# Four edits to the first half of a fused attention and two-layer-block kernel: later exponentials and casts, one copy joined, six staging tiles

## The chip, the cores and the metric

One core of a Trainium2 chip runs the whole program. The metric is device time in microseconds (us) of one execution. The kernel before took 992.32 us (median of 3 runs, 990.58 to 995.51).

## The reference

Three stages follow one another. (1) Causal attention with forgetting, for 4 batches of 8 heads, 576 tokens, head size 64: scores are `q·k / 8` plus a decay `cum[i] - cum[j]` (`cum` is the running sum of `log f`), the upper triangle is masked, and each row is turned into weights by `exp(score - row max)`, divided by its sum, and multiplied with `v`. (2) With the heads side by side (2304 tokens of 512): `h = x @ w_in` (2048 wide), `g = h * tanh(softplus(h))`, `x = g @ w_out`. (3) `a = x @ w1`, `b = x @ w2` (1024 wide each), `out = ((a * b) @ w3) @ w_out2`. All weights of the two blocks come as 64-bit floats and are turned into 32-bit ones on the chip.

## The kernel before

**Two halves.** `phase_a` does the attention of 16 pairs of heads, converts all weights, multiplies w3 with w_out2 beforehand, and computes `h = x @ w_in` for three of the four batches. `phase_b` computes `h` for the last batch and then the rest of blocks (2) and (3) on token quarters. The change is in the first half; the second is touched only where both halves share `l1_unit`.

**Slots.** The first half is a loop over 68 slots, four for each pair of heads `p` (lines 675 to 706, the four are numbered j = 0 to 3). A head's rows are cut into five blocks, called c = 0 to 4; a score block c has 128 rows of both heads, the last has 64 rows of each head in one tile. In slots j = 0, 1, 2 the scores of blocks (0, 1), (2, 3) and (4) are computed. At the end of slots j = 1, 2, 3 and of the next pair's slot 0, `turn` transposes blocks (0, 1), (2), (3) and (4) on TensorE and copies them out of PSUM. So a block is transposed a slot or more after its exponentials. In slot j = 3 the product with `v` (`pv`) of the pair before is made, scaled by VectorE (`x_rows`), and split into a high and a low part (`x_parts`: two casts on ScalarE, two subtractions on GpSimd).

**Fillers.** TensorE's order is written out by hand. Between scores and transposes each slot runs filler matmuls in two bursts (lines 697 to 702). From slot 21 on they are first-layer units: 12 matmuls give one 128 x 288 block of `h` in one of two PSUM banks (`ps_l`), ScalarE copies it into a staging tile `h`, and SyncE stores the tile to memory (`h_scr`). There are two units in a slot, one for each burst, 24 matmuls of line 512. There are `HB = 3` staging tiles. A unit can start only when the unit two before it has been copied out of its bank.

**Softmax of a block.** Line 357 (363 and 364 for block 4): VectorE adds the mask, scales and takes the row minimum. Line 367: ScalarE takes the exponential in place and sums the row (an ACTIVATE and a read of the accumulator). Both are called from `score`, before the first filler burst.

**Conversions.** Each 1024-word piece of a weight is loaded into a raw tile (line 117, four buffers of the tag `cvr`, names cvrt for w3, cvri for w_in, cvru for w_out, cvrv for w1 and w2), ScalarE makes the exponent part (line 132, `cv_exp`), VectorE puts the bits together (lines 140 to 142, `cv_bits`), and then the raw tile is free. `job` puts the load at slot s-1 and the two steps one or two slots after s. The loads go over SyncE's queue, together with the stores of `h`. From slot 47 on one load is issued for each buffer that comes free.

**Order on the other engines.** The orders of ScalarE, VectorE, GpSimd and SyncE are fixed when the program is built: a planner goes through it in time with estimated durations, and when an engine is free it takes the ready instruction with the highest priority. Priority is the place in the program, moved ahead by an offset: 200 for the scores, the softmax and `cv_exp`, 150 for the copies of `h`, 100 for the transposes and their copies, 50 for `pv`, `x_rows` and `x_parts`. On the chip each engine then works strictly in that order.

**First-layer order of batch 0.** `l1_all` takes both halves of the tokens for the first `L1_BOTH = 10` weight columns m, then half 0 of the remaining six, then half 1 of them.

Of the kernel before, what the change touches and what calls it, by code (L numbers as in the profile page):

```python
# [9 lines left out]
F32 = mybir.dt.float32  # L10
F32R = mybir.dt.float32r
BF16 = mybir.dt.bfloat16
I32 = mybir.dt.int32
AF = mybir.ActivationFunctionType
# [10 lines left out]
TB = S // 2  # L25
# [10 lines left out]

HB = 3
CV = 4
HP_L1 = 150
HP_ATT = 100  # L40
HP_SM = 200
HP_PV = 50
# [3 lines left out]
W3_STEP = 1.14  # L46
WP_END = 21
W_IN_SLOT = 16
L1_BOTH = 10
W_IN_STEP = 0.8  # L50
W_OUT_SLOT = 30
W_OUT_STEP = 1.08
# [22 lines left out]
class Kernel:  # L75
# [38 lines left out]

    def cv_load(self, key, src, where=None):
        if where is None:
            raw = self.att.tile([128, 1024], I32, name=f"cvr{key}", tag="cvr", bufs=4)
        else:
            raw = self.w_tile(where, f"cvr{key}", I32)
        dst = raw if len(src.shape) == 2 else raw.rearrange("p (c w) -> p c w", c=src.shape[1])  # L120
        self.nc.sync.dma_start(dst, src)
        self.cv[key] = [raw, None]

    def cv_exp(self, key):
# [3 lines left out]
        else:  # L128
            t = self.att.tile([128, 512], F32, name=f"cv{key}", tag="cv", bufs=CV)
        self.cv[key][1] = t  # L130
# [209 lines left out]
                mm(ps[:, 512 * part:512 * part + TB], t[:, LAST:LAST + 128], t[:, TB * part:TB * part + TB],  # L340
                   start=first, stop=not first)

    def softmax(self, p, c):
        nc = self.nc
        ps = self.S.pop((p, c))
        if c == 0:
            self.sums = self.att.tile([128, 16], F32, name=f"sum{p}", tag="sum", bufs=2)
        ttr = nc.vector.tensor_tensor_reduce
        self.nsm = self.nsm % 6 + 1
        st = [self.sums[:, 8 + self.nsm:9 + self.nsm]]  # L350
        if c < 4:
            n = 128 * (c + 1)
            P = self.P[c]
            self.nsm = self.nsm % 6 + 1
            st.append(self.sums[:, 8 + self.nsm:9 + self.nsm])
            for hh in range(2):
                dve = ttr(P[hh][:, :n], ps[:, 512 * hh:512 * hh + n], self.m1[:, 512 - n:], -0.125, 3.0e38, ALU.add,
                          ALU.min, st[hh])
            cols = (c, 5 + c)
        else:  # L360
            n = S
            P = self.P[4]
            ttr(P[0][:, :TB], ps[:, :TB], self.m1[:, :TB], -0.125, 3.0e38, ALU.add, ALU.min, self.sums[:, 15:16])
            dve = ttr(P[0][:, TB:n], ps[:, 512:512 + TB], self.m4, -0.125, self.sums[:, 15:16], ALU.add, ALU.min, st[0])  # L364
            cols = (4,)
        for t, b, i in zip(P, st, cols):
            ins = nc.scalar.activation(t[:, :n], t[:, :n], AF.Exp, bias=b, scale=-1.0, accum_out=self.sums[:, i:i + 1])  # L367
        return ins, dve

    def inv_sums(self):  # L370

# [39 lines left out]
    def pt_parts(self, p, c, hh):  # L411

        nc = self.nc
        copy = nc.vector.tensor_copy if hh else nc.scalar.copy
        dst = self.pt[:, 2 * (p % 2) + hh]
        if c < 4:
            o = self.t_col(c)
            src = self.ps_t[hh][:, o:o + 128 * (c + 1)].rearrange("p (k q) -> p k q", q=128)
            return copy(dst[:, 0:c + 1, 128 * c:128 * c + 128], src)  # L419
        src = self.ps_t[0].rearrange("p (k q) -> p k q", q=128)  # L420
        if not hh:
            copy(self.pt4[p % 2][0:64], self.ps_t[1][0:64, 0:128])
        return copy(dst[:, :, 512:576], src[:, :, 64 * hh:64 * hh + 64])

    def pv(self, p):
        mm = self.nc.tensor.matmul
# [38 lines left out]
    def wp_unit(self, f):  # L465
# [5 lines left out]
        def step(g, k, i):  # L471
# [7 lines left out]
            if i == 23:  # L479
                t = self.cv[2, f % 4, f // 4] = self.w_tile(0, f"wp{f}", F32)[:, :512]  # L480
                with self.tc.high_priority(offset=HP_L1):
                    self.nc.scalar.copy(t, o)
# [17 lines left out]
    def l1_unit(self, b, m, half):  # L500
        mm = self.nc.tensor.matmul
        steps = []
        box = []

        def step(c, k, i):
            if i == 0:
                box.append(self.l1_bank())
            o = box[0]
            a, bb = MM_PAIRS[k]
            w = self.wi[m][:, 512 * a + 128 * c:512 * a + 128 * c + 128]  # L510
            x = self.X[4 * b + c, half][:, TB * bb:TB * bb + TB]
            mm(o[:, :TB], w, x, start=i == 0, stop=i == 11)  # L512
            if i == 11:
                t = self.base.tile([128, TB], F32, name=f"h{b}_{m}_{half}", tag="h", bufs=HB)
                with self.tc.high_priority(offset=HP_L1):
                    if self.late_l1:
                        self.nc.vector.tensor_copy(t, o[:, :TB])
                    else:
                        self.nc.scalar.copy(t, o[:, :TB])  # L519
                self.nc.sync.dma_start(self.h_scr[128 * m:128 * m + 128, b * S + TB * half:b * S + TB * half + TB], t)  # L520

        i = 0
        for c in range(4):
            for k in range(3):
                steps.append(((f"i{m}",), lambda c=c, k=k, i=i: step(c, k, i)))
                i += 1
        return steps

    def l1_all(self, b):
        out = []  # L530
        units = [(m, half) for half in range(2) for m in range(DFF // 128)]
        if b == 0:

            units = [(m, half) for m in range(L1_BOTH) for half in range(2)]
            units += [(m, half) for half in range(2) for m in range(L1_BOTH, DFF // 128)]
        for m, half in units:
# [28 lines left out]
    def phase_a(self):  # L565
        nc = self.nc
# [55 lines left out]
        for i in range(32):  # L622
            f = i % 16
            s = W_OUT_SLOT + int(W_OUT_STEP * i)
# [7 lines left out]
            else:  # L632
                key, src = f"v{f}", self.cols((self.w1, self.w2)[f % 2], f // 2)
                job(s, key, src, self.cv_store, key, self.w12_scr[f], lag=2)
        for p in range(NPAIR):
            s = NU * p
# [8 lines left out]

        for f in FS:
            self.filler.extend(self.wp_unit(f))
        self.S, self.nsm, self.act, self.dve = {}, 0, None, None
        with self.tc.manual_schedule(engines={mybir.EngineType.PE}):
            self.slots(misc, conv, self.plan())  # L650
        self.psp.__exit__(None, None, None)
# [1 line left out]
        self.lowp.__exit__(None, None, None)  # L653

    def slots(self, misc, conv, cnt):

        def turn(p, cs):
            with self.tc.high_priority(offset=HP_ATT):
                for c in cs:
                    self.transposes(p, c)  # L660
                if cs == (4,):
                    self.nc.tensor.transpose(self.ps_t[1][0:9, 384:512], self.inv, self.ident)
                    self.inv_rows(p)
                for c in cs:
                    self.act = self.pt_parts(p, c, 0)
                    self.dve = self.pt_parts(p, c, 1)

        def score(p, cs):
            with self.tc.high_priority(offset=HP_SM):
                for c in cs:  # L670
                    self.scores(p, c)
                for c in cs:
                    self.act, self.dve = self.softmax(p, c)

        for s in range(NU * (NPAIR + 1)):
            self.slot = s
            self.done |= self.fresh
            self.fresh.clear()
            if s in L1_S:
                self.filler.extend(self.l1_all(L1_S.index(s)))  # L680
            p, j = divmod(s, NU)
            n = cnt[s]
            live = p < NPAIR
            with self.tc.high_priority(offset=HP_SM):
                for key in conv.get(s, []):
                    self.cv_exp(key)
            if live and j < 3:
                score(p, ((0, 1), (2, 3), (4,))[j])
            if p and j == (3 if live else 2):
                with self.tc.high_priority(offset=HP_PV):  # L690
                    self.pv(p - 1)
                    self.x_rows(p - 1)
                    self.x_parts(p - 1)
            with self.behind(self.dve):
                for key in conv.get(s, []):
                    self.cv_bits(key)
            k = n // 2 if s < WP_END else n // 24 * 12
            self.run_filler(k)
            with self.behind(self.act):
                for fn, a in misc.get(s, []):  # L700
                    fn(*a)
            self.run_filler(n - k)
            if p and j == 0:
                turn(p - 1, (4,))
            elif live and j:
                turn(p, ((0, 1), (2,), (3,))[j - 1])
        while self.filler and len(self.filler) % 12:
            self.filler.popleft()[1]()
# [387 lines left out]
```

## Time and profile before

| | |
|---|---|
| median of 3 runs | 992.32 us |
| profiled execution | 990.14 us, span 988.4 us |
| busy over the span: TensorE, VectorE, ScalarE, GpSimd | 91%, 62%, 50%, 42% |
| mean granted clock of TensorE | 0.979 of 2.4 GHz |

A busy share is a mean over stages with different limits; the first half runs up to about 447 us of the span. A wait row says which engine and line waited for which. A row of the timeline shows the start, the duration, the engine, the line and the tiles, and in brackets the idle time ahead of it and what ended it.

### The profile page before, as it was taken

The numbers are of one execution on the slowest core, as the hardware profiler recorded it, in microseconds if no ns is written. First come the engines' busy times: TensorE is split into PE (matmuls) and PEld (weight loads), VectorE is DVE, ScalarE is ACT, GpSimd is POOL, SyncE is SP. The second block draws the span as 40 slices with busy tenths as digits, with TensorE's granted clock in tenths as the row PEclk, the third lists the DMA queues.
The fourth block names the chain that finished last, engine by engine and source line by source line (L and its number), as shares of the span: only waits on it lengthen the run. The fifth ranks groups of instructions, "written<-read, shape, count | busy, mean of one in ns | idle before, by whom it ended". The sixth has DMA issues, their size and how long they took to land.

```text
span 988.4 us, 17836 instructions
## 1 busy us (share of the span) xinstructions
PE 901.1 (91%) x6432; PEld 827.2 (84%) x6432; DVE 610.0 (62%) x1051; ACT 491.1 (50%) x1091; POOL 410.4 (42%) x403
## 2 busy tenths in 40 slices
PE   0699999899989889997899897999999899999998
PEld 0467667788878777897899897999999899999998
DVE  5987677645666454522358649766559944744462
ACT  1666676656667554526213545543755344422143
POOL 4757677416666500001014568453154454400042
PEclk9899999999999989999799999999999999999999
DMA  8457667747998885538565454855986435455552
GB/s 252 142 164 236 215 207 232 240 140 232 293 302 288 280 274 182 180 123 346 193 234 166 131 193 148 306 183 184 398 278 201 164 129 170 151 162 160 169 173 73
DMA packets 138439, 204.89 MB, mean 207 GB/s; under 512 B 13344, under 2 KB 80304, under 8 KB 138352
## 3 DMA queue, kind: packets, MB, share of 16 engines
q1 hardware_dynamic: 138352, 203.76, 63.1%
q8 instruction: 51, 0.84, 0.4%
q14 instruction: 36, 0.29, 0.1%
HBM read 138.76 MB, written 64.86 MB: 206 GB/s over the span
## 4 chain that ended last, share of the span: by engine, by line
PE 50%; DVE 6%; DMA 4%; issue 1%; ACT 1%; SPq 0%; DVEq 0%; ACTq 0%
PE ps_x L881 12%; PE ps_x L953 10%; PE ps_y L881 6%; PE ps_z L881 6%; PE ps_z L953 5%; PE ps_l L512 4%; PE ps_y L953 2%; PE ps_x L512 2%; DMA y<-h_scr 2%; DMA cvrv<-in_w_dram 1%; DVE g_l L862 1%; PE ps_z L512 1%; DMA h_scr<-h 1%; PE ps_s L437 1%; DVE y L855 1%
## 5 line engine op out<-in xcount | busy, mean ns | idle before, releaser
L512 PE MATMUL ps_l<-x,wi 128*128 128x288 f32 x1152 | 171.1, 306 | 14.6 <-ACT h L519 14.6
L512 PEld LDWEIGHTS ps_l<-x,wi 128*128 128x128 f32 x1152 | 160.2, 195 | 26.7 <-ACT h L519 20.0
L862 POOL TENSOR_TENSOR g_l<-y,g_h 128x576 fp32r<-128x576 f32 x48 | 74.2, 1549 | 126.4 <-PE ps_y L512 52.7
L860 ACT CAST g_h<-y 128x576 fp32r<-128x576 f32 x96 | 63.9, 674 | 85.3 <-PE ps_y L512 31.5
L881 PE MATMUL ps_x<-g_h,ws 128*128 128x288 f32 x512 | 93.3, 301 | 2.4 <-ACT g_h L860 2.1
L862 POOL TENSOR_TENSOR h_l<-ab,h_h 128x576 fp32r<-128x576 f32 x24 | 35.5, 1480 | 126.1 <-ACT h_h L860 115.1
L367 ACT ACTIVATE P<-P,sum 128x256 f32<-128x256 f32 (+3 forms) x112 | 70.4, 631 | 23.6 <-DVE sum L364 11.9
L862 DVE TENSOR_TENSOR g_l<-y,g_h 128x576 fp32r<-128x576 f32 x48 | 53.6, 1120 | 44.7 <-ACT g_h L860 44.2
L881 PEld LDWEIGHTS ps_x<-g_h,ws 128*128 128x128 f32 x512 | 77.8, 193 | 3.5 <-ACT g_h L860 2.8
L111 POOL TENSOR_TENSOR x<-xx,x 128x288 fp32r<-128x288 f32 x32 | 29.5, 942 | 119.7 <-ACT x L97 90.2
L881 PE MATMUL ps_x<-g_l,ws 128*128 128x288 f32 x256 | 56.9, 304 | 11.1 <-DVE g_l L862 8.3
L336 PE MATMUL ps_s<-raw 64*128 64x128 f32 (+3 forms) x256 | 50.8, 475 | 9.8 <-DMA raw<-in_qk_dram 5.4
L419 DVE COPY pt<-ps_t 128x128 f32<-128x128 f32 (+1 forms) x64 | 29.7, 484 | 48.6 <-PE ps_t L404 47.5
L953 PE MATMUL ps_x<-T,gs 128*128 128x288 f32 x384 | 54.5, 296 | 2.1 <-ACT C L958 1.2
L953 PE MATMUL ps_x<-T,ws 128*128 128x288 f32 x384 | 54.4, 296 | 2.3 <-ACT x L911 1.4
L336 PE MATMUL ps_s<-aug 64*128 64x128 f32 (+3 forms) x128 | 36.7, 557 | 21.5 <-DMA aug<-pt 21.5
L953 PEld LDWEIGHTS ps_x<-T,gs 128*128 128x128 f32 x384 | 52.1, 189 | 2.8 <-ACT C L958 1.5
L953 PEld LDWEIGHTS ps_x<-T,ws 128*128 128x128 f32 x384 | 52.0, 189 | 2.9 <-ACT x L911 1.7
L519 ACT COPY h<-ps_l 128x288 f32<-128x288 f32 x96 | 36.5, 392 | 35.5 <-PE ps_l L512 18.6
L881 PEld LDWEIGHTS ps_x<-g_l,ws 128*128 128x128 f32 x256 | 42.3, 194 | 13.0 <-DVE g_l L862 9.7
L860 ACT CAST h_h<-ab 128x576 fp32r<-128x576 f32 x48 | 31.9, 673 | 36.4 <-PE ps_x L881 17.6
L478 PE MATMUL ps_l<-wo,w3h 128*128 128x512 f32 x128 | 45.3, 423 | 4.8 <-POOL wo L111 3.1
(226 smaller groups left out, 2264.3 us busy)
## 6 DMA issues: line engine op xcount, KB each, us to landing
ws<-ws SPq DMA_DIRECT2D x112, 512.0 KB
h_scr<-h SPq DMA_DIRECT2D x128, 144.0 KB
y<-h_scr SPq DMA_DIRECT2D x32, 576.0 KB
ws<-gs SPq DMA_DIRECT2D x56, 256.0 KB
ws<-pt SPq DMA_DIRECT2D x48, 256.0 KB
ws<-bs SPq DMA_DIRECT2D x36, 256.0 KB
cvrt<-in_w3t_dram SPq DMA_DIRECT2D x16, 512.0 KB
cvri<-in_w_in_dram SPq DMA_DIRECT2D x16, 512.0 KB
```

The source lines that it names most:

```text
L111: ins = self.nc.gpsimd.tensor_tensor(lo[..., c], raw[..., c], f32(hi[..., c]), ALU.subtract)
L336: mm(ps[:, 512 * hh:512 * hh + n], t[r, q0:q0 + 128], t[r, 0:n], start=first, stop=not first)
L367: ins = nc.scalar.activation(t[:, :n], t[:, :n], AF.Exp, bias=b, scale=-1.0, accum_out=self.sums[:, i:i + 1])
L419: return copy(dst[:, 0:c + 1, 128 * c:128 * c + 128], src)
L437: mm(ps[64 * hh:64 * hh + 64, 256 + q:256 + q + w], lhs, rhs, start=i == 0, stop=i == len(plan) - 1)
L478: mm(o, w, x, start=i == 0, stop=i == 23)
L512: mm(o[:, :TB], w, x, start=i == 0, stop=i == 11)
L519: self.nc.scalar.copy(t, o[:, :TB])
L860: self.nc.scalar.copy(hi, raw)
L862: eng.tensor_tensor(lo, raw, f32(hi), ALU.subtract)
L881: mm(ps[:, r, :TB], w[:, 256 * a + 128 * e:256 * a + 128 * e + 128], ops[i][b][:, r], start=o in (1, 5, 2) and f == 0 and (a, b) == (0, 0) ...
L953: mm(bank[:, r, :TB], w[:, 256 * a + 128 * k:256 * a + 128 * k + 128], T[o, k][:, b, r], start=o in (1, 2, 5) and (k, a, b) == (0, 0, 0), ...
```

## The change

The exponentials leave `softmax` (now `smax`, which only remembers what they need) and become `exps`, called behind the first filler burst with the offset 50. `x_parts` moves from its place next to `pv` into the list of the slot's other work, also behind the first burst, without an offset. For block 4 of a pair, ScalarE no longer copies its half of the transposed tile: VectorE copies both heads in one instruction (128 x 512), and ScalarE keeps the small 64 x 128 copy. In the first half `h` alternates between three tiles of the old pool and three new ones, and the raw tiles go from four to three. `L1_BOTH` goes from 10 to 6.

```diff
+CVR = 3
+HA = 3
-L1_BOTH = 10
+L1_BOTH = 6
@@ cv_load
-            raw = self.att.tile([128, 1024], I32, name=f"cvr{key}", tag="cvr", bufs=4)
+            raw = self.att.tile([128, 1024], I32, name=f"cvr{key}", tag="cvr", bufs=CVR)
@@
-    def softmax(self, p, c):
+    def smax(self, p, c):
...
-        for t, b, i in zip(P, st, cols):
-            ins = nc.scalar.activation(t[:, :n], t[:, :n], AF.Exp, bias=b, scale=-1.0, accum_out=self.sums[:, i:i + 1])
-        return ins, dve
+        self.E[c] = [(t[:, :n], b, self.sums[:, i:i + 1]) for t, b, i in zip(P, st, cols)]
+        return dve
+
+    def exps(self, c):
+        for t, b, total in self.E.pop(c):
+            ins = self.nc.scalar.activation(t, t, AF.Exp, bias=b, scale=-1.0, accum_out=total)
+        return ins
@@ pt_parts
-        src = self.ps_t[0].rearrange("p (k q) -> p k q", q=128)
         if not hh:
-            copy(self.pt4[p % 2][0:64], self.ps_t[1][0:64, 0:128])
-        return copy(dst[:, :, 512:576], src[:, :, 64 * hh:64 * hh + 64])
+            return copy(self.pt4[p % 2][0:64], self.ps_t[1][0:64, 0:128])
+        i = 2 * (p % 2)
+        src = self.ps_t[0].rearrange("p (k h q) -> p h k q", h=2, q=64)
+        return copy(self.pt[:, i:i + 2, :, 512:576], src)
@@ l1_unit
-                t = self.base.tile([128, TB], F32, name=f"h{b}_{m}_{half}", tag="h", bufs=HB)
+                pool = self.base if self.late_l1 or self.nl1 % (HB + HA) < HB else self.att
+                t = pool.tile([128, TB], F32, name=f"h{b}_{m}_{half}", tag="h", bufs=HB if pool is self.base else HA)
@@ slots
-                    self.act, self.dve = self.softmax(p, c)
+                    self.dve = self.smax(p, c)
...
-            if live and j < 3:
-                score(p, ((0, 1), (2, 3), (4,))[j])
+            units = ((0, 1), (2, 3), (4,), ())[j] if live else ()
+            if units:
+                score(p, units)
             if p and j == (3 if live else 2):
                 with self.tc.high_priority(offset=HP_PV):
                     self.pv(p - 1)
                     self.x_rows(p - 1)
-                    self.x_parts(p - 1)
+                at(s, self.x_parts, p - 1)
...
             self.run_filler(k)
+            with self.tc.high_priority(offset=HP_PV):
+                for c in units:
+                    self.act = self.exps(c)
             with self.behind(self.act):
```

## Rows read from the trace of the kernel before

**Rows 1.** Windows by stage: length, busy time (instructions) of each engine, granted clock, DMA

```profile
55.00:147.00 92.00, 86.44 (x538) 63.48 (x536) 68.87 (x168) 62.95 (x182) 62.33 (x74) 1.00 0.67 206
147.00:389.00 242.00, 225.91 (x1660) 194.72 (x1656) 146.60 (x366) 151.16 (x452) 115.07 (x143) 0.97 0.79 248
389.00:447.00 58.00, 56.50 (x439) 50.62 (x440) 22.87 (x55) 23.35 (x69) 4.70 (x6) 1.00 0.45 150
447.00:480.00 33.00, 23.40 (x146) 22.22 (x145) 9.26 (x18) 21.07 (x19) 1.45 (x2) 0.81 0.87 340
480.00:988.40 508.40, 486.42 (x3587) 481.47 (x3585) 318.74 (x361) 209.14 (x322) 197.06 (x129) 0.99 0.56 187
```

**Rows 2.** Waits of PE, 147 to 447 us: total, times, longest

```profile
PE ps_l L512 <- ACT h L519: 14.6, 14, 2.5
```

**Rows 3.** Waits of ACT, 40 to 447 us: total, times, longest

```profile
ACT cvv L132 <- DMA cvrv<-in_w_dram: 29.7, 12, 5.5
ACT x L97 <- DVE xx L445: 24.9, 12, 3.3
...
ACT h L519 <- DMA h_scr<-h: 10.9, 7, 5.5
ACT cvi L132 <- DMA cvri<-in_w_in_dram: 10.0, 7, 3.1
```

**Rows 4.** Timeline of ACT, then of PE: two stalls behind exponentials

```profile
177.02 0.62 ACT L367 ACTIVATE P<-P,sum 128x384 f32<-128x384 f32 x1
...
179.65 0.37 ACT L519 COPY h<-ps_l 128x288 f32<-128x288 f32 x1
...
180.08 3.48 PE L512 MATMUL ps_l<-x,wi 128*128 128x288 f32 x24 [0.50 <-ACT h L519]
...
413.42 3.47 PE L512 MATMUL ps_l<-x,wi 128*128 128x288 f32 x24 [0.44 <-ACT h L519]
```

**Rows 5.** Timeline of ACT and PE: a load, an exponential, a copy

```profile
360.29 0.67 ACT L132 ACTIVATE cvv<-cvrv 128x512 f32<-128x512 f32 x1 [2.75 <-DMA cvrv<-in_w_dram]
360.86 0.70 ACT L367 ACTIVATE P<-P,sum 128x512 f32<-128x512 f32 x1
...
362.00 4.83 PE L512 MATMUL ps_l<-x,wi 128*128 128x288 f32 x24 [2.45 <-ACT h L519]
```

**Rows 6.** Window behind that stall, and two pairs of units on PE

```profile
362.00:367.00 5.00, 5.00 (x28) 5.00 (x29) 0.40 (x1) 1.85 (x6) 0.00 (x0) 0.70 0.83 273
...
187.00 3.45 PE L512 MATMUL ps_l<-x,wi 128*128 128x288 f32 x24
...
173.96 3.74 PE L512 MATMUL ps_l<-x,wi 128*128 128x288 f32 x24 [1.59 <-ACT h L519]
```

**Rows 7.** Timeline of ACT: a copy of h that waits for a store

```profile
327.14 0.40 ACT L519 COPY h<-ps_l 128x288 f32<-128x288 f32 x1 [5.50 <-DMA h_scr<-h]
```

**Rows 8.** Timeline of SP and ACT: two raw loads and their exponent steps

```profile
276.41 0.40 SPq L121 DMA_DIRECT2D cvru<-in_w_out_dram  x1
...
298.77 0.68 ACT L132 ACTIVATE cvu<-cvru 128x512 f32<-128x512 f32 x1 [0.35 <-POOL bs L799]
...
398.22 0.43 SPq L121 DMA_DIRECT2D cvrv<-in_w_dram  x1
...
402.05 0.68 ACT L132 ACTIVATE cvv<-cvrv 128x512 f32<-128x512 f32 x1 [2.47 <-DMA cvrv<-in_w_dram]
```

**Rows 9.** Timeline of POOL and PE: the last w_in column, later units

```profile
210.00 1.44 POOL L111 TENSOR_TENSOR wi<-cvi,wi 128x256 fp32r<-128x256 f32 x2 [3.21 <-ACT wi L97]
...
214.06 3.45 PE L512 MATMUL ps_l<-x,wi 128*128 128x288 f32 x24
```

**Rows 10.** Groups by line and shape: copies of transposed block 4

```profile
L419 DVE COPY pt<-ps_t 128x512 f32<-128x512 f32 x16 | 10.9, 684 | 23.3 <-PE ps_t L404 23.3
...
L423 DVE COPY pt<-ps_t 128x256 f32<-128x256 f32 x16 | 6.8, 422 | 51.4 <-ACT pt L423 51.4
...
L423 ACT COPY pt<-ps_t 128x256 f32<-128x256 f32 x16 | 6.0, 372 | 0.0
```

More of the change, by code (lines that the diff above doesn't have):

```diff
@@ L647, in phase_a @@
             self.filler.extend(self.wp_unit(f))
-        self.S, self.nsm, self.act, self.dve = {}, 0, None, None
+        self.S, self.E, self.nsm, self.act, self.dve = {}, {}, 0, None, None
         with self.tc.manual_schedule(engines={mybir.EngineType.PE}):
@@ L655, in slots @@
     def slots(self, misc, conv, cnt):
+        at = self.at
         def turn(p, cs):
```

## The prediction

> **What bounds the kernel now.** I read the windows by stage first, then who waited for whom on TensorE, then the instructions around single stalls. In the windows [rows 1] TensorE is busy for 86.4 of 92 us before 147 us, for 225.9 of 242 us from there to 389, and for nearly all of the 58 us after that. So the first half is bound by TensorE with small holes, and the holes sit where first-layer units run: 242 - 225.9 = 16.1 us. After 447 us comes a stretch of 33 us in which TensorE works 23.4 us while 340 GB/s flow; that is the change-over to the second half, which the change does not aim at. The waits of TensorE name one cause: 14 waits, 14.6 us together, in which a matmul of line 512 stands because ScalarE has not yet copied `h` out of the bank that it needs [rows 2]. ScalarE isn't short of time (151 of 242 us busy [rows 1]); the copy stands in its queue behind something else. What that is shows in its own waits: it waits for raw loads (29.7 us for w1 and w2, 10.0 us for w_in), for `xx` (24.9 us), and for stores that must land before a staging tile is free (10.9 us) [rows 3].
>
> **Sorting the 14 stalls.** I went through them by the ScalarE instructions that end just before the copy.
> - Five stand behind a run of exponentials: 0.50, 0.90, 0.46, 1.16 and 0.45 us, 3.5 us together. The first and the last are in [rows 4]. In the first, exponentials run from 177.02 to the copy at 179.65, though the unit's last matmul was long past; the stall ends at 180.08.
> - Six stand behind a mixture: a load or another wait, then one or two exponentials or the casts of `x`, then the copy; 7.5 us. [rows 5] is the longest: ScalarE waits 2.75 us for a load, converts 0.67, takes an exponential 0.70 (and 0.19 for its sum, less the overlap), and TensorE has stood 2.45 us. What the exponentials and casts hold of these six is 0.46 + 1.37 + 0.66 + 0.28 + 0.70 + 0.66 = 4.1 us.
> - One, 1.4 us, is the copy that waits 5.50 us for a store [rows 7].
> - Two, 2.2 us, have neither.
>
> **Exponentials and casts later.** The copies of `h` have the offset 150, the exponentials fall from 200 to 50 and the casts of `x` from 50 to none, so where both are ready the copy goes first. The first group goes whole and the second by its 4.1 us: 7.6 us. What waits for the exponentials? They stand behind a burst of 12 matmuls, half of the 3.45 us of a pair of units [rows 6], so 1.7 us later; behind them on ScalarE are the slot's casts and the copies of transposed blocks. A block is transposed a slot or more later, and a slot takes 300 us / 45 = 6.7 us (147 to 447 us hold slots 21 to 65). Some 1.7 us plus four exponentials of about 0.9 stay under that, so I price the delay at nothing; if ScalarE fell a slot behind, each transposition would stall by what is missing. The bounds of this edit are 0, if the planner goes on placing exponentials first because they are ready first, and all 14.6 us.
>
> **The clock.** After the stall at 359.5 us the granted clock is 0.70 in the 5 us that follow [rows 6], that is, part of the time at 1.2 GHz. The 24 matmuls there take 4.83 us [rows 5] against 3.45 [rows 6]: 1.4 us more. Three stalls, of 2.0 to 2.5 us, are followed by this, some 4.3 us in all; the stall of 1.59 us is followed by 3.74 us, 0.3 more. Taking exponentials and casts out leaves two of the three at about 1.4 and 1.75 us. A stall that is shortened but still followed by the slow stretch gives nothing back here. I count 2.2 us of gain, one and a half of three, between 0 and 4.3. The Trainium skill ("TensorE: Matmul & The Clock Gate", Terms) puts the penalty at the throttled time times the missing share of the clock; for this stretch that is an estimate of 5.0 x 0.30 = 1.5 us. The trace agrees with 1.4 us; by the page's price the three would be 4.5 us in place of 4.3.
>
> **Six staging tiles.** ScalarE's 10.9 us of waits for stores [rows 3] go. On TensorE only the one stall of 1.4 us showed; I take 1.4, between 0 and 2.8 (one more of the two without a cause). Each store is still issued by SyncE in order, with the same bytes. In the second half the tiles are the old three, so the change-over is priced at 0; it takes 33 us [rows 1] whatever came before.
>
> **Three raw tiles.** This is the edit that costs. Each load starts when a raw tile comes free, so with three it starts about one job later, close to a slot (6.7 us). For w_out the exponent step comes 298.77 - 276.41 = 22.4 us after the load's issue [rows 8]; 22.4 - 6.7 is still far over the 3.8 us in which a load lands (398.22 to 402.05). No new wait there. For w1 and w2 the step already waits for the load, 12 times of 16. For w_in it waits 7 times of 16, 1.4 us each [rows 3]; if it becomes 16, ScalarE waits 9 x 1.4 = 13 us more. What does that cost TensorE? Of the 29.7 us in the w1 and w2 stage, the stalls that would be left are 2.0 and 1.75 us with one or two slow stretches, about 6 us, a fifth. A fifth of 13 is 2.6; I take 2.8. Bounds: 0, and everything, 13 plus four more waits of 2.5 in the last stage, 23 us. Before 147 us TensorE feeds on other fillers and hides ScalarE's waits (86.4 of 92 us busy [rows 1]).
>
> The Trainium skill ("Perfetto Trace Analysis", Optimization Strategy) says that the same gap repeating on the engine that should be saturated can mean too few buffers for the next tile. That speaks for six staging tiles and against three raw tiles; its second half is the slower rival below.
>
> **Batch 0 order.** With 6 in place of 10, column 15 is needed in unit 21 and not in 25 (counted from 0). Unit 21 is the second of the pair that starts at 214.06, so at 215.8; the column's low part is ready at 211.44 [rows 9]. The 4.4 us between are eaten by gains in front of it (0.46 + 1.37 + 0.50 + 0.66 and one slow stretch, 4.4). I take 1 us of new stall; bounds 0 and a slot, 6.7.
>
> **Block 4's copy.** VectorE's copy grows from 422 to about 684 ns (the same size in line 419), ScalarE loses 372 [rows 10]. VectorE waited for ScalarE's half, so the pair ends 0.37 + 0.42 - 0.68 = 0.1 us sooner. The product that reads it comes three slots later, so 0; at most 16 x 0.1 = 1.6 us either way.
>
> **Sum.** -7.6 - 2.2 - 1.4 + 2.8 + 1 = -7.4 us. The profiled execution took 990.14 us (span 988.4 and 1.7 around it), so 982.7; the median of runs is 2.2 us above the profiled one, so **985 us**.
>
> **Rivals.**
> - *The order hardly moves.* The planner takes whatever is ready when ScalarE is free, and an exponential is ready about when the first unit ends. Then only a quarter of 7.6 comes: -1.9 - 1.4 + 2.8 + 1 = +0.5, 993 us. For it: in [rows 4] nothing but time separates them. Against it: at 179.65 a finished unit plainly waited behind exponentials of higher priority.
> - *Raw tiles set the pace (slower).* Place: ScalarE's exponent step, in front of the copies of `h`. It decides if three releases come so late that a load is issued less than its 3.8 us before the step, for w_in and w_out as it is now for w1 and w2. That last stage has 7.2 us of stalls and two slow stretches of 1.45, 10.1 us over 16 conversions, 0.63 each. For 32 more that is 20 us in place of my 2.8: 985 - 2.8 + 20 = 1002 us. For it: 402.05 waited 2.47 us although there were four tiles [rows 8]. Against: the 22.4 us of the w_out row.
> - *All of it goes.* No stall behind `h` copies, no slow stretch, no cost: -14.6 - 4.3, 973 us. For it: ScalarE has 91 of 242 us free [rows 1]. Against: two stalls have no part in the edits.
>
> **How the numbers follow.** Forecast 0.46 (its own range 979 to 990), order hardly moves 0.22, raw tiles 0.21, all goes 0.11. A measurement of this kernel tells 0.5% (5 us) from no change, so the borders are 987.4 and 997.3. Faster: 0.39 of the forecast's share and all of the last, 0.50. Slower: the raw tiles with 0.03 of the second, 0.24. Same: 0.26. The range runs from 974 to 1002; it leaves out the half of the last rival that lies lower and the worse half of the slower one.
>
> **What would show it.** Right: the wait of line 512 for line 519 falls from 14.6 to about 5.6 us, ScalarE's waits for stores to about 0, its waits for w_in loads rise from 10 to over 20 us, the last product of line 437 comes some 7 us sooner, and the second half keeps its length. Wrong: ScalarE's load waits rise and TensorE's waits for line 519 do not fall (raw tiles), or copies of `h` still end runs of exponentials (order). The prediction fails in another way if the change-over at 447 us, with its 33 us, gets longer or shorter.

## The result, and the profile after

The changed kernel takes 1002.18 us (median of 18 runs, 994.84 to 1006.47), the kernel before 993.78 (18 runs): 1.0079 times as long, 95% interval 1.0059 to 1.0099. It is slower by 0.8% where 985 us was forecast. The profiled execution took 1000.65 us, its span 998.9, against 990.14 and 988.4.

First, in which half the 10.5 us lie. The first half ends where the first unit of the last batch starts on TensorE (the tile is called `ps_z` there). The timeline of PE has it, for the kernel after:

```profile
454.00 1.85 PE L519 MATMUL ps_z<-x,wi 128*128 128x288 f32 x12 [1.01 <-DVE xx L452]
```

and for the kernel before:

```profile
445.03 1.81 PE L512 MATMUL ps_z<-x,wi 128*128 128x288 f32 x12 [1.01 <-DVE xx L445]
```

The first half is 9.0 us longer, and the rest 544.9 against 543.4 us: 9.0 of the 10.5 us are lost in the first half. These are its windows after, with the columns of [rows 1]:

```profile
55.00:147.00 92.00, 85.99 (x519) 63.22 (x520) 68.03 (x165) 59.69 (x172) 61.85 (x73) 0.96 0.63 194
147.00:389.00 242.00, 221.45 (x1627) 190.61 (x1626) 141.76 (x354) 146.44 (x437) 112.02 (x144) 0.96 0.78 246
```

From 147 to 389 us TensorE is busy for 221.5 us where it was 225.9, with 33 matmuls fewer, so the same work is later. Up to 147 us little is lost in sum: a window over that stretch holds 604 matmuls, against 608 before. But the granted clock of its last 92 us is 0.96, where the kernel before had 1.00 [rows 1]; why is seen further down. Who waited for whom, on PE from 147 to 447 us:

```profile
PE ps_l L519 <- ACT h L527: 22.3, 15, 4.3
PE ps_s L338 <- DVE xx L452: 2.3, 1, 2.3
```

The wait that the change was to shorten has grown from 14.6 us [rows 2] to 22.3. ScalarE's waits from 40 to 447 us say why:

```profile
ACT cvv L134 <- DMA cvrv<-in_w_dram: 39.4, 12, 5.0
ACT cvi L134 <- DMA cvri<-in_w_in_dram: 20.9, 11, 5.2
ACT x L99 <- DVE xx L452: 18.7, 9, 3.2
...
ACT cvu L134 <- DMA cvru<-in_w_out_dram: 11.3, 4, 4.2
ACT cvt L134 <- DMA cvrt<-in_w3t_dram: 8.9, 6, 2.5
```

The rows for `h` stores have gone, as they should with six staging tiles. But all four kinds of raw load are waited for longer: 80.5 us together. Before it was 49.0: the two rows in [rows 3] and, not shown there,

```profile
ACT cvt L132 <- DMA cvrt<-in_w3t_dram: 5.7, 4, 2.0
...
ACT cvu L132 <- DMA cvru<-in_w_out_dram: 3.6, 2, 1.9
```

How such a wait reaches TensorE is seen at the place of the first stall of [rows 4], in the timelines of SP, ACT and PE after:

```profile
175.29 0.44 SPq L123 DMA_DIRECT2D cvri<-in_w_in_dram  x1
...
180.53 0.69 ACT L134 ACTIVATE cvi<-cvri 128x512 f32<-128x512 f32 x1 [3.18 <-DMA cvri<-in_w_in_dram]
181.11 0.61 ACT L373 ACTIVATE P<-P,sum 128x384 f32<-128x384 f32 x1
...
183.02 0.71 ACT L373 ACTIVATE P<-P,sum 128x512 f32<-128x512 f32 x1
...
183.72 0.38 ACT L527 COPY h<-ps_l 128x288 f32<-128x288 f32 x1
...
184.16 5.01 PE L519 MATMUL ps_l<-x,wi 128*128 128x288 f32 x24 [2.03 <-ACT h L527]
```

and the window behind it:

```profile
184.20:189.20 5.00, 5.00 (x26) 5.00 (x27) 0.76 (x2) 3.35 (x9) 4.07 (x6) 0.66 0.75 229
```

This is the thirteenth load of w_in. With three raw tiles it must wait for the bit steps of the tenth, which end on VectorE with

```profile
172.14 0.69 DVE L144 SCALAR_TENSOR_TENSOR cvi<-cvri,cvi 128x512 int32<-128x512 int32 x1
```

So the tile is free at 172.83. SyncE then issues three other transfers first, and the load only at 175.29. ScalarE stands 3.18 us for it. Behind it come the same four exponentials as before, still ahead of the copy of `h`, and TensorE stalls 2.03 us. Then the granted clock is 0.66 for 5 us, and 24 matmuls take 5.01 us in place of 3.45 [rows 6].

The same happens ahead of 147 us, where the load of a w_in piece holds up the copy of a transposed block; these are ACT, PE, and a window behind the stall:

```profile
116.16 0.66 ACT L134 ACTIVATE cvi<-cvri 128x512 f32<-128x512 f32 x1 [5.19 <-DMA cvri<-in_w_in_dram]
...
117.25 1.09 PE L410 MATMUL ps_t<-ident,P 128*128 128x128 f32 x8 [1.50 <-ACT pt L425]
...
122.00:127.00 5.00, 5.00 (x18) 3.81 (x18) 0.39 (x3) 3.20 (x12) 3.82 (x7) 0.55 0.28 80
```

The longest stall of all, however, stands behind a wait of another kind. ScalarE's exponent step needs a tile for its result too, one of four, and that tile must first have been stored (`w_scr`):

```profile
348.42 1.22 ACT L134 ACTIVATE cvv<-cvrv 128x512 f32<-128x512 f32 x2 [5.88 <-DMA w_scr<-cvv]
...
350.65 5.47 PE L519 MATMUL ps_l<-x,wi 128*128 128x288 f32 x24 [4.25 <-ACT h L527]
```

In the kernel before this wait was 1.8 us, and TensorE's stall at this point of the program 1.98. The 5.88 us are not among the 80.5.

So two things are to be explained: why ScalarE waits longer, and why the exponentials have not moved.

### The profile page after: what moved, and what is told of

It reads as the page before. It is cut to its first block, busy times and chain, and to the rows that moved or that the text cites. A ratio compares the mean times of both kernels' runs of the same rounds, so it can differ in the third digit from the quotient of the medians.

```text
span 998.9 us, 17843 instructions
## 1 busy us (share of the span) xinstructions
PE 903.9 (90%) x6432; PEld 829.7 (83%) x6432; DVE 611.5 (61%) x1051; ACT 486.4 (49%) x1075; POOL 407.9 (41%) x403
## 4 chain that ended last, share of the span: by engine, by line
PE 61%; DMA 14%; DVE 10%; issue 5%; ACT 5%; POOL 4%; SPq 1%; DVEq 0%; ACTq 0%; POOLq 0%
PE ps_x L895 12%; PE ps_x L967 9%; PE ps_l L519 9%; PE ps_y L895 6%; PE ps_z L895 6%; PE ps_z L967 5%; PE ps_s L338 3%; DMA y<-h_scr 2%; PE ps_y L967 2%; DMA cvrv<-in_w_dram 2%; PE ps_x L519 2%; PE ps_l L485 2%; ACT P L373 2%; DMA cvri<-in_w_in_dram 2%; PE ps_s L444 1%
## 5 line engine op out<-in xcount | busy, mean ns | idle before, releaser
L519 PE MATMUL ps_l<-x,wi 128*128 128x288 f32 x1152 | 170.8, 306 | 22.3 <-ACT h L527 22.3
L359 DVE CUSTOM_DVE_ANT_0 P<-ps_s,m 128x256 f32<-128x256 f32 (+2 forms) x96 | 49.5, 553 | 7.5 <-PE ps_s L338 7.2
```

## The experiments

Theory: with three raw tiles loads start later, ScalarE stands for them at the head of its queue, and the other edits give back little. Rival: the moved exponentials themselves put ScalarE's queue in a worse order. Each kernel ran five rounds beside the kernel before, which had a median of 994.07 us in the runs beside experiments 1 to 4, 990.68 beside 5 to 8 and 992.43 beside 9 to 12. Ratios, with 95% intervals, are to the kernel before in the same set, and are not simply the quotient of two medians. "PE's waits" are those for copies of `h` from 147 to 447 us, "load waits" those of ScalarE for the four kinds of raw loads from 40 to 447 us; both come from one profiled execution each, the ratios from many.

**1. Three raw tiles alone.** In the kernel before:

```diff
-            raw = self.att.tile([128, 1024], I32, name=f"cvr{key}", tag="cvr", bufs=4)
+            raw = self.att.tile([128, 1024], I32, name=f"cvr{key}", tag="cvr", bufs=3)
```

> The kernel before with three raw tiles in place of four, nothing else. Theory (raw tiles): most of the 8 us of loss is here, ratio 1.006 to 1.014; ScalarE's waits for w_in loads rise from 10 to about 20 us and the waits of first-layer matmuls for h copies to over 20 us. Rival (order: the later exponentials and casts cost it): ratio 0.998 to 1.002.

1.0064 (1.0035 to 1.0093). Waits of PE, then of ACT:

```profile
PE ps_l L512 <- ACT h L519: 25.4, 18, 4.4
...
ACT cvv L132 <- DMA cvrv<-in_w_dram: 37.4, 11, 5.0
...
ACT cvi L132 <- DMA cvri<-in_w_in_dram: 19.2, 13, 3.3
...
ACT cvu L132 <- DMA cvru<-in_w_out_dram: 11.2, 4, 4.3
ACT cvt L132 <- DMA cvrt<-in_w3t_dram: 9.7, 4, 3.0
```

One number of the old kernel gives most of the loss, and the rows of the changed kernel nearly one for one.

**2. Three raw tiles and six staging tiles**, experiment 1 with

```diff
-                t = self.base.tile([128, TB], F32, name=f"h{b}_{m}_{half}", tag="h", bufs=HB)
+                pool = self.base if self.late_l1 or self.nl1 % (HB + HA) < HB else self.att
+                t = pool.tile([128, TB], F32, name=f"h{b}_{m}_{half}", tag="h", bufs=HB if pool is self.base else HA)
```

> The kernel before with three raw tiles and six staging tiles (both memory edits, no other). Theory: slower by about as much as with the raw tiles alone, the staging tiles giving back 1 to 3 us: ratio 1.003 to 1.012; ScalarE's waits for stores of h at 0. Rival (order): 0.996 to 1.001.

1.0064 (1.0038 to 1.0091), the same as without the staging tiles, although ScalarE's waits for stores fell to one of 1.2 us (6.5 us in experiment 1). In the time, those waits were hidden. PE's waits are 18.0 us in the profile of this kernel, 7.4 less than in experiment 1, but it was taken in the fastest of the ten runs (994.27 us, their median is 999.04), and the two medians are 0.1 us apart.

**3. Only the exponentials and the casts of `x` moved**, with four raw and three staging tiles: of the change's diff the parts `smax`, `exps` and `slots`, and

```diff
+            with self.tc.high_priority(offset=HP_PV):
+                for c in units:
+                    self.act = self.exps(c)
```

> The kernel before with exponentials and casts of x behind the first burst, nothing else (four raw tiles, three staging tiles, L1_BOTH 10, block 4 in two copies). Theory: faster or the same, ratio 0.992 to 1.000, since the copies of h no longer stand behind exponentials. Rival (order costs): 1.004 to 1.010.

1.0013 (0.9989 to 1.0037): nothing. PE's waits are 14.5 us, as before. I then compared the order of ScalarE's instructions in the two profiles, buffer numbers and the reads of the accumulator left out: 945 of 947 stand in the same sequence, and the two that moved are steps of conversions. Runs of four exponentials directly ahead of a copy of `h` are 11 in both. The edit is in the source and hardly in the program.

**4. The changed kernel with four raw tiles**, and three staging tiles, since six do not fit beside four raw ones:

```diff
-CVR = 3
+CVR = 4
...
-                pool = self.base if self.late_l1 or self.nl1 % (HB + HA) < HB else self.att
+                pool = self.base
```

> The changed kernel with four raw tiles and, because both don't fit, three staging tiles: order of exponentials and casts, joined copy and L1_BOTH 6 stay. Theory: the loss is gone, ratio to the kernel before 0.992 to 1.001. Rival (order or L1_BOTH): still 1.004 to 1.010.

0.9989 (0.9964 to 1.0015). The loss is gone, PE's waits are 16.9 us. What is left of the change, the joined copy and the order of batch 0 included, is worth nothing that can be measured, either way.

**5. Exponentials forced behind a copy of `h`.** Experiment 4, with an ordering edge to the copy of the slot's first unit:

```diff
-            with self.tc.high_priority(offset=HP_PV):
+            with self.behind(self.hcopy), self.tc.high_priority(offset=HP_PV):
                 for c in units:
                     self.act = self.exps(c)
```

> The changed kernel with four raw tiles and three staging tiles, and a written order edge: a slot's exponentials are queued behind the copy of h of the slot's first unit, which the offsets alone did not bring about. Theory (stalls behind exponentials are worth what the prediction said): waits of first-layer matmuls for h copies fall from about 15 to 8 us or less, ratio to the kernel before 0.988 to 0.995. Rival (the same stalls come back behind loads): the waits stay over 12 us, ratio 0.997 to 1.003.

1.003 (1.0004 to 1.0056): my expectation failed and the rival's held. Runs of four ahead of a copy fell to 7, so now the order did change, and PE's waits are still 14.0 us. ScalarE now stands for the unit, and still for the loads:

```profile
ACT h L528 <- PE ps_l L520: 28.4, 21, 2.9
ACT cvv L135 <- DMA cvrv<-in_w_dram: 27.2, 11, 5.8
```

So as long as the loads stand in front, exponentials ahead of copies are a mark of the stalls and not what sets the time. (Experiment 11 takes them away with the loads gone.)

**6. The exponent step put last.** If the harm is that ScalarE stands for a load ahead of the copies, the step has to move, not the exponentials. Experiment 4, with `cv_exp` taken from the head of the slot and queued behind its exponentials:

```diff
-            with self.tc.high_priority(offset=HP_SM):
-                for key in conv.get(s, []):
-                    self.cv_exp(key)
...
+            with self.behind(self.act), self.tc.high_priority(offset=HP_PV):
+                for key in conv.get(s, []):
+                    self.cv_exp(key)
```

(`cv_bits`, the bit steps on VectorE, follows it, so it moves too, and the offset of the exponent step falls from 200 to 50. The three were not run apart.)

> The changed kernel with four raw tiles and three staging tiles, and the exponent step of the conversions queued on ScalarE behind the slot's exponentials in place of ahead of them. Theory (ScalarE stands at its queue's head for loads): its waits for raw loads fall from about 50 to under 25 us and TensorE's waits for h copies with them, ratio 0.985 to 0.996. Rival (the loads only come later by as much, since raw tiles come free later): load waits stay over 40 us, ratio 0.998 to 1.006.

0.9857 (0.9829 to 0.9885), 977.92 us. ScalarE waits for no raw load any more, and PE's waits are 11.6 us.

**7. Two raw tiles** in the kernel before (`bufs=2`).

> The kernel before with two raw tiles. Theory (raw tiles): the loss grows with each tile taken away, ScalarE's waits for raw loads over 100 us, ratio 1.015 to 1.06. Rival (what three tiles cost is an accident of one order of the queues): 0.998 to 1.008.

1.014 (1.0105 to 1.0175). The loss grows with every tile taken away, but less than expected: the ratio lies just under the 1.015 to 1.06, load waits came to 88.7 us and not over 100, and PE's waits (24.4 us) did not grow over those of experiment 1. Where the rest of the loss lies was not followed up.

**8. The whole change, the exponent step put last.** Three raw and six staging tiles, with the edit of experiment 6.

> The changed kernel, three raw and six staging tiles, with the exponent step of the conversions queued on ScalarE behind the slot's exponentials. Theory (the loss is ScalarE standing at a load ahead of the copies of h): most of the loss goes, ratio to the kernel before 0.990 to 1.002. Rival (the conversions themselves come too late with three tiles, and their readers wait): still 1.005 to 1.015.

0.9853 (0.9825 to 0.988), 977.49 us. It cannot be told from experiment 6 with four raw tiles. Its waits of PE, and the one row for raw loads among those of ACT:

```profile
PE ps_l L519 <- ACT h L527: 9.9, 9, 4.9
...
ACT cvi L134 <- DMA cvri<-in_w_in_dram: 0.5, 2, 0.3
```

Its windows:

```profile
55.00:147.00 92.00, 90.68 (x564) 67.73 (x563) 72.82 (x171) 62.30 (x180) 67.61 (x76) 0.98 0.68 210
147.00:389.00 242.00, 228.39 (x1723) 196.60 (x1723) 150.58 (x370) 150.02 (x450) 119.40 (x144) 0.99 0.82 256
```

Its timeline, at the place looked at above (ACT) and at the end of the first half (PE):

```profile
174.18 0.71 ACT L373 ACTIVATE P<-P,sum 128x512 f32<-128x512 f32 x1
...
174.89 0.38 ACT L527 COPY h<-ps_l 128x288 f32<-128x288 f32 x1
175.17 1.24 ACT L134 ACTIVATE cvi<-cvri 128x512 f32<-128x512 f32 x2
...
432.76 1.81 PE L519 MATMUL ps_z<-x,wi 128*128 128x288 f32 x12 [1.01 <-DVE xx L452]
```

At 174.89 the copy of `h` still ends a run of exponentials, but the exponent step now stands behind it, twice in a row, and its loads are there. The load waits are 0.5 us in place of 80.5, with the same three tiles. (Half of the 9.9 us of PE's waits is one stall, which three raw tiles keep: at 341.70, 4.89 us, behind a wait of 5.07 us for the store to `w_scr`. That wait is 5.1 to 6.5 us in five of the six profiles with three raw tiles, and 3.8 or less in all with four.) From 147 to 389 us the clock is 0.99 (0.96 in the changed kernel), and 96 matmuls more are done than there; in the 92 us ahead of that it is 45 more. The first half ends 21.2 us sooner than in the changed kernel.

What the edit bought shows when each load's issue on SyncE is set against its exponent step on ScalarE. Call the time between them the load's lead. For w1 and w2 its median is 5.6 us in the kernel before, 5.1 in the changed kernel and 12.7 here; for w_in it is 6.9, 5.2 and 9.5. So the load has landed when the step comes. The step isn't out of the way of the copies: directly ahead of one it stands 17 times here and 11 times in the changed kernel (147 to 447 us). It only no longer waits there. Nor does ScalarE stand less in all: its waits for VectorE's row minima, ahead of the exponentials, go from 19.0 to 54.0 us.

**9. The kernel before, the exponent step put last**, with nothing else of the change.

> The kernel before with one edit: the exponent step of the conversions queued on ScalarE behind the slot's exponentials; four raw and three staging tiles, exponentials where they were. Theory (loads at the head of ScalarE's queue were the stalls all along): 0.983 to 0.991, load waits under 10 us. Rival (the gain needs the moved exponentials of the change too): 0.993 to 1.002.

0.9877 (0.9854 to 0.9901), 980.23 us; no waits for raw loads, and store waits up from 10.9 to 18.5 us. Its waits of PE, and its windows:

```profile
PE ps_l L512 <- ACT h L519: 10.0, 14, 1.9
...
55.00:147.00 92.00, 89.47 (x559) 66.10 (x558) 70.28 (x172) 63.84 (x185) 68.04 (x75) 1.00 0.68 210
147.00:389.00 242.00, 231.59 (x1736) 197.96 (x1734) 153.08 (x372) 150.40 (x459) 121.21 (x145) 0.99 0.82 256
```

These rows account for the gain of some 12 us: PE's waits are 4.6 us less; the clock of the 242 us goes from 0.97 to 0.99, some 4.8 us; and a window up to 147 us holds 19 matmuls more (627 against 608), at 225.9 / 1660 = 0.136 us each 2.6 us. The last two are estimates from the windows, and the clock's is a rough one: each granted clock is rounded to 0.01, which is 2.4 us of the 242.

**10. Experiment 8 with the old order of batch 0** (`L1_BOTH = 10`).

> The changed kernel with the exponent step behind the exponentials (three raw, six staging tiles) and L1_BOTH back at 10. Theory: the batch-0 order costs or gives nothing that can be measured, within 0.003 of the same with 6 (0.9853). Rival (order of batch 0 cost the 1 us and more that the prediction gave it): 0.981 or lower.

0.9834 (0.9812 to 0.9857), 975.91 us: the fastest version that ran, though its interval overlaps that of experiment 8. With the step last, the order of batch 0 makes no difference that can be measured.

**11. Experiment 8 with the exponentials forced** as in experiment 5.

> The changed kernel (three raw, six staging tiles) with the exponent step behind the exponentials and the exponentials forced behind the copy of h of the slot's first unit. Theory (with the loads gone the exponentials are the next thing ahead of the copies): 0.975 to 0.984. Rival (ScalarE then waits in order for the unit and stalls elsewhere): 0.985 to 0.995.

0.986 (0.9835 to 0.9885). Waits of PE, then of ACT:

```profile
PE ps_s L339 <- DVE xx L453: 8.7, 4, 4.1
PE ps_l L520 <- ACT h L528: 2.1, 5, 1.1
...
ACT h L528 <- PE ps_l L520: 57.8, 34, 3.9
```

PE's waits for copies are almost gone, and the time is the same: part came back as waits of the scores for `xx`, so a smaller wait row was no gain. ScalarE's load waits are 13.1 us here, in four waits.

**12. The same with four raw and three staging tiles.**

> As the one before with four raw and three staging tiles. Theory: within 0.003 of it, since with the step out of the way neither the raw tiles nor the staging tiles count. Rival (staging tiles count once copies come early): slower than it by 0.005 or more.

0.9855 (0.9835 to 0.9875). ScalarE's store waits are 36.1 us here (21 waits), the largest of any kernel, and cost nothing.

## Why the prediction was wrong

The forecast took 11.2 us of credit from later exponentials, the clock and six staging tiles, and none of it came; and it charged 2.8 us for the raw tile taken away, which cost some 6 to 9.

The slower rival, "raw tiles set the pace", named the place, ScalarE's exponent step ahead of the copies, and its price of 1002 us is the time measured. That the number fits is luck: two errors cancel in it. It priced the raw tiles at 20 us, against a credit of 10 us from the other edits that did not come. And its condition, a load issued less than 3.8 us before the step, isn't what the rows show: the load of 175.29 was issued 5.2 us before and waited for.

- **Exponentials and casts later (-7.6): failed.** The step assumed that lower offsets would put the copies first. The written order did not change (experiment 3), as the rival "the order hardly moves" said; its reason, that the planner takes what is ready when ScalarE is free, fits but was not tested by itself. And where an edge forced the order (5), nothing was gained, so sorting the stalls by the last instruction ahead of the copy was wrong too. Every instruction between the wait and the copy shares in the delay; I charged the nearest ones. By experiments 8 and 9 part of the charge belongs to the load's wait, as the 2.75 us of [rows 5]: PE's waits fall by 12.4 of 22.3 us and by 4.6 of 14.6. Some 10 us of them are left in both with hardly a load waited for. In experiment 8, 4.9 of that is the stall behind the store to `w_scr`; what sets the rest was not looked for, and experiment 11 shows that most of it can go without a gain in time.
- **The clock (-2.2): failed with it.** The reading of a slow stretch held: after stalls of 2.03 to 4.25 us in the changed kernel 24 matmuls took 4.97 to 5.47 us. But they did not get fewer: three followed stalls for copies of `h` of some 2 us and more, as in the kernel before, and one that it did not have came at 117 to 127 us, behind the stall for a transposed block. One stall of 2.76 us was followed by 3.44 us, and in the kernel before one of 0.28 us by 4.98, so a stall's length alone does not tell it.
- **Six staging tiles (-1.4): nothing.** Store waits went, as forecast; experiment 2 shows no gain in time.
- **Three raw tiles (+2.8): the term that was mis-sized.** Alone it cost 1.0064, some 6 us; between experiment 4 and the changed kernel, which also differ in staging tiles, the ratio is 1.0079 / 0.9989 = 1.0090, some 9 us, and the intervals overlap. Two parts of the step were off. ScalarE waits 31.5 us more and not 13: w_in 10.9, as forecast (over 20 us in all), but w1 and w2 9.7, w_out 7.7 and w3 3.2. "No new wait" for w_out came from one load with a lead of 22.4 us [rows 8]. Loads did come close to a slot later there (the median lead of the 16 falls from 20.3 to 12.9 us), but the first four never had the room: their leads were 5.2 to 8.2 us in the kernel before. In the changed kernel one was issued at 202.90 and used at 207.29 after a wait of 4.23. PE's waits grew by 7.7 us against these 31.5, a quarter, near the fifth that I took. But 2.3 of the 7.7 are the growth of the stall at 350 us, and its wait for the store to `w_scr` stands nowhere in the step; the slow stretches came on top.
- **"Before 147 us TensorE feeds on other fillers and hides ScalarE's waits": only in part.** In that stretch of 92 us experiments 8 and 9 fill 90.7 and 89.5 us where 86.4 were busy [rows 1]. 5.6 us of holes were too many to pass over. And in the changed kernel a load wait of 5.19 us at 116 us reached TensorE, with 5 us at a clock of 0.55 behind it.
- **Batch 0's order (+1): nothing.** The last column was ready at 219.34 and unit 21 started at about 219.9; nearly all of the 4.4 us of margin had been eaten, none of it overdrawn.
- **Block 4's copy (0): right.** VectorE's joined copy takes 691 ns (684 was the estimate). It was not run alone; it lies within the 0.9989 of experiment 4.
- **The second half: right.** 544.9 against 543.4 us.

What the working lacked is the question that experiments 6, 8 and 9 answer: which instruction stands at the head of an in-order queue and waits. ScalarE was free for 91 of 242 us [rows 1], so it seemed to have room; but at 180.53 four exponentials and a copy stand behind its wait for a load. With that step last, three raw tiles do as well as four, to the 0.3% that the intervals allow. So the loss from the raw tile taken away is shown to hang on the place of the waiting step. Shown as well is that the step, come later, finds its load landed. Not shown is why the load itself is issued when it is: the tile came free late, and SyncE had other transfers in front; the two were not taken apart. The Trainium skill ("Perfetto Trace Analysis", Optimization Strategy) says that a gap repeating on the engine that should be saturated can mean too few buffers; the runs agree as long as the step stands first (1.0064 with three tiles, 1.014 with two), and no longer once it stands last (0.9853 with three, 0.9857 with four).

## What to carry to other kernels

When a busy engine waits for a copy, follow the copier's queue back past the work in between to the first instruction that waited, and ask whether it can come later, so that what it waits for is there: here that move gave 1.2% alone. Six staging tiles and other priorities gave nothing, and the fourth raw tile was worth 0.6% only as long as the step stood first. Before pricing a change of priorities, compare the orders that come out. And price a buffer taken away by the leads of all loads that use it, the shortest first.

## What the runs showed that was not expected

Raw loads that ScalarE waited for took 3.8 us from issue to use in [rows 8], 4.4 for the one issued at 202.90 and 5.2 for the one at 175.29. The total flow doesn't sort them: in these three stretches it was 275, 191 and 301 GB/s. What does stays open. And waits on TensorE can be taken away with no gain: 9.9 us in experiment 8 and 2.1 in experiment 11 go with times that cannot be told apart.
